# A residual quantizer on one core: the score sums laid out by row group, and the list schedule's numbers that go with it

## The chip, the cores and the metric

The kernel runs on one core of one Trainium2 chip. Time is device time in microseconds (us) of one execution; a kernel's time is the median over its runs. A profiled execution also leaves a trace, in which every instruction of every engine has a start and a duration. The engines are PE (matrix multiply), DVE (vector), ACT (scalar and activations), POOL (used for memsets, small copies and to issue stores) and SP (used to issue loads).

## The reference

The input x has 2 sequences of 16000 rows with 512 bf16 values each. Every row is convolved over time with 3 taps per value and passed through silu. Four quantizer stages follow, each with 8 codes of 512 values: a stage picks the code that is nearest to the residual, adds it to q and takes it from the residual. At the end q is convolved with 3 other taps.

```python
z = silu(sum(xp[:, i:i+T, :] * dw_enc[i] for i in range(3)))
res, q = z, 0
for s in range(4):
    cb = codebooks[s]                                     # 8 x 512
    d2 = sum(res*res)[..., None] - 2 * res @ cb.T + sum(cb*cb)
    sel = cb[d2.argmin(-1)]
    q, res = q + sel, res - sel
y = sum(qp[:, i:i+T, :] * dw_dec[i] for i in range(3))
```

## The kernel before

**Tiles.** A tile is G row groups of 128 partitions, G = 16 for 14 of the 18 tiles and 6 or 8 for the two first and two last. Row p x G + g of the tile is partition p of group g once a row's data lie across the partitions; for the convolution and the residual the 512 values lie on the partitions instead (4 chunks of 128) and the rows along the free dimension (tile ZB).

**Stages of a tile n.** `load` (L456) has SP transpose rows into XT. `front` (L473) multiplies by the taps (L491 on DVE, L490 on ACT), adds (TA, then ZB, both through the helper `tt`, whose instructions all carry L333), and takes exp on ACT (L496) and one plus that on DVE (L498). `front2` (L501) takes the reciprocal on ACT (L508) and multiplies on DVE (ZB<-ZB,EX at L333). `select` (L541) gets from PE, per row, the squared norm and the products with the codes of all stages (L526; read out on DVE at L562 into rr and at L563 into S), and then decides stages 0 to 2 one after another. `resid` (L642) takes the three picked codes off ZB on PE (L661, L662), with the result read out by ACT (L668) or by DVE (L670), then gets the products of the last stage (L688, L689) and decides it (L694 to L699). `windows` (L624) transposes the picks (OHA) on PE (L633) and copies them to OHW (L639). `back` (L704) multiplies OHW by codes that already carry the taps (L721 to L725); ACT reads the result out into YB (L729) and POOL stores it (L752).

**A decision.** For stage s, with shapes of 128 partitions x G row groups x 8 codes:
- PR gets a stage's score without the norm: from S at stage 0 (L573), from RC at stage 1 (L580), from PE's correction in PSUM plus S at stage 2 (L583), and for the last stage as a copy of 8 row groups at a time from PSUM (L689). The arithmetic is f32 in, bf16 out.
- V = PR + the rounded norm (TR at L585, rr3 at L694), bf16 from bf16.
- KEY's upper half-words = V + CCB, the codes' own norms (L588, L696). KEY is f32; its lower half-words hold the code's number, so that no two scores are equal. This instruction writes every second half-word.
- M = the least KEY of each row group (L589, L697), OHA = KEY equal to M (L594, L698).
- For the next stage, PE transposes OHA (L600), ACT or DVE copies that to OT (L604, L605), and PE multiplies it with the codes' products (corr, L610), for RC at L578 or PR at L583; the picked score E (L614, via L333) and its sum RD (L616) update the norm.

PR and V are laid out code by row group: eight runs of GM = 16 values. Instructions that go row group by row group see them through a turned view:

```python
VT, PT = W["V"][:, :, 0:G], W["PR"][:, :, 0:G]                  # [P, C, G], as they lie
V, PR = VT.rearrange("p c g -> p g c"), PT.rearrange("p c g -> p g c")
```

L585 and L694 run in the order in which they lie (the norm then has a step of 1 in the inner loop, over row groups); all others that touch PR or V run through the turned view, with 32 bytes from one code to the next.

**What sets the order.** No engine's order is written out. Each operation is given to `Plan.add` with an engine (or the choice of two), a cost, and a key of stage, tile and place within it. `Plan.order` (L56) is a list scheduler: it keeps a clock for each engine and each PSUM bank and repeatedly takes the operation that could start first by its costs, with ties broken by `rank` (L52), a weighted sum of tile number and place in the stage. WHEN (L213) holds these weights per stage, for first, middle and last tiles (the first 3 and the last 3 are apart). SHARE (L210) shifts the choice between ACT and DVE for the read-out of `resid`, SLACK (L211) for the other operations that either may do (taps, plus 1, OT, OHW). The engines then run their instructions in that order, each waiting for its inputs by semaphores. The scheduler's costs are estimates in the source; the time on the chip doesn't depend on them except through the order.

Of the kernel before, what the change touches and what calls it, by code (L numbers as in the profile page):

```python
# [8 lines left out]
BF16 = mybir.dt.bfloat16  # L9
# [169 lines left out]
def kernel(  # L179
# [8 lines left out]
    nc = tc.nc  # L188
# [18 lines left out]
    PAIR = 1  # L207
    NX, NE, NZ, NOH, NY = 2, 3, 4, 4, 4
    NA = 4
    SHARE = (6.37, 3.09, -1.14)  # L210
    SLACK = (0.29, -1.21, -11.84)  # L211
    QUOTA = {"ACT": 3, "DVE": 4}
    WHEN = {"setup": ((0.48, 0.203), (1.124, 0.191), (0.894, 0.256)), "load": ((-1.978, 0.928), (-1.958, 0.788), (-1.958, 0.928)),  # L213
            "pad": ((-1.401, 0.11), (-1.77, 0.139), (-2.325, 0.134)), "taps": ((-0.057, 0.383), (-0.336, 0.394), (0.031, 0.912)),
            "exp": ((1.263, 0.221), (1.069, 0.366), (0.904, 0.173)), "plus1": ((0.866, 0.996), (0.171, 0.587), (-0.047, 0.932)),
            "recip": ((1.611, 0.712), (1.323, 0), (2.178, 0.449)), "gate": ((0.117, 0.508), (1.051, 0.495), (1.918, 0.485)),
            "score0": ((-0.068, 0.062), (1.311, 0.496), (0.173, 0.112)), "decide": ((1.738, 0.411), (0.985, 0.17), (0.833, 0.78)),
            "win0": ((2.163, 0), (1.992, 0), (2.9, 0.025)), "resid": ((1.585, 0.812), (1.683, 0.698), (1.981, 0.795)),
            "score3": ((2.128, 0.491), (2.581, 0.216), (3.162, 1.381)),
            "decide3": ((0.792, 0.352), (0.868, 0.614), (1.912, 0.464)), "win3": ((2.95, 0.386), (2.949, 1.184), (3.689, 0.225)),  # L220
            "back": ((2.837, 0.461), (3.158, 0.814), (4.316, 0.502))}
    assert B == len(SIZES) and T >= GM * P and GM <= 16

    xf = x.flatten_outer_dims()
# [22 lines left out]
    def sb(shape, dt, name):  # L247
        return const.tile(list(shape), dt, name=name)
# [24 lines left out]
    YB = [sb([P, 4, D], BF16, f"YB{b}") for b in range(NY)]  # L273
    WDBC = YB[3][:, 0:K, :]
    SS = [{"S": sb([P, GM, N3], F32, f"S{b}"), "rr": sb([P, 3, GM, 1], F32, f"rr{b}"), "RD": sb([P, 2, GM, 1], F32, f"RD{b}"),
           "TR": sb([P, 3, GM, 1], BF16, f"TR{b}"), "RC": sb([P, GM, C], F32, f"RC{b}"), "PR": sb([P, C, GM], BF16, f"PR{b}"),
           "V": sb([P, C, GM], BF16, f"V{b}"), "M": sb([P, GM, 1], F32, f"M{b}"), "E2": sb([P, GM, C], F32, f"E2{b}"),
           "OT": [sb([GCM, P], BF16, f"OT{b}_{s}") for s in range(2)],
           "PR3": sb([P, C, GM], BF16, f"PR3{b}"), "rr3": sb([P, GM, 1], BF16, f"rr3{b}"),
           "V3": sb([P, C, GM], BF16, f"V3{b}"), "M3": sb([P, GM, 1], F32, f"M3{b}")} for b in range(2)]  # L280
    PS = [psum.tile([P, 1024], F32, name=f"ps{b}") for b in range(NA)]
    NPART = 3
    BIG = float(2.0 ** 100)
# [257 lines left out]
    def select(st):  # L541
# [1 line left out]
        GC = G * C  # L543
        b = n % 2
        W = SS[b]
        S, M, RC, E2 = W["S"][:, 0:G], W["M"][:, 0:G], W["RC"][:, 0:G], W["E2"][:, 0:G]
        VT, PT = W["V"][:, :, 0:G], W["PR"][:, :, 0:G]
        V, PR = VT.rearrange("p c g -> p g c"), PT.rearrange("p c g -> p g c")
        rr = [W["rr"][:, j, 0:G] for j in range(3)]
        TR = [W["TR"][:, j, 0:G] for j in range(3)]  # L550
        RD = [W["RD"][:, j, 0:G] for j in range(2)]
# [16 lines left out]
        for s in range(3):  # L568
# [6 lines left out]
            else:  # L575
# [6 lines left out]
                else:  # L582
                    add("DVE", small, key(0), lambda pc=pc, cs=cs: nc.vector.tensor_tensor(out=PR, in0=pc(), in1=S[:, :, cs], op=ALU.add),  # L583
                        [("S", b)], [("PR", b)], free=pbox, after=[pj])
            tt(VT, PT, TR[s].rearrange("p g o -> p o g").to_broadcast([P, C, G]), ALU.add, dve(GC, 1.92), key(1), [("PR", b), ("TR", b, s)], [("V", b)])  # L585
            KY = KEY[0]
            k16 = KY.bitcast(BF16).rearrange("p g (c h) -> p g c h", h=2)
            tt(k16[:, 0:G, :, 1], V, CCB[:, :, cs].to_broadcast([P, G, C]), ALU.add, small, key(2), [("V", b), "CCB"], [("KEY", 0)])  # L588
# [35 lines left out]
    def windows(st, s0, s1, key):  # L624
        n, GH = st["n"], st["GH"]
        A, W = OHA[n % NOH], OHW[n % NOH]
        box = {}

        def trans():
            pwb = ps(box).bitcast(BF16)  # L630
            for k in range(GH):
                for s in range(s0, s1):
                    nc.tensor.transpose(pwb[NC * s:NC * (s + 1), k * P:(k + 1) * P],  # L633
                                        A[:, s, 2 * k:2 * k + 4, :].rearrange("p g c -> p (g c)"), IDENT)
        r = slice(NC * s0, NC * s1)
        j = add("PE", 0.5 + GH * 0.0125, key, trans, [("OHA", n % NOH), "I"], [], take=("S", box), mm=GH * (s1 - s0))
        dst = W[r, 0:GH, PADC:PADC + P]
        src = lambda: ps(box).bitcast(BF16)[r, 0:GH * P].rearrange("p (k c) -> p k c", c=P)
        either({"ACT": act_psum(GH * P), "DVE": dve(GH * P, 1.92)}, key, lambda: nc.scalar.copy(dst, src()), lambda: nc.vector.tensor_copy(dst, src()),  # L639
               [], [("OHW", n % NOH, s0 // 3)], free=box, after=[j])  # L640

    def resid(st):  # L642
        n, G, GH = st["n"], st["G"], st["GH"]
        Z, W = ZB[n % NZ], OHW[n % NOH]
        m = 0
        for s in range(3):
            for u in range(2):
                for i in range(KT):
                    box = {}
                    key = ("resid", n, m / 24)  # L650
                    m += 1
                    zg = Z[:, i, u:G:2, :]
                    tok = ("Z", n % NZ, i, u)

                    def mms(s=s, u=u, i=i, zg=zg, box=box):
                        on_act = box["dest"] == "ACT"
                        for k0 in range(0, GH, 4):
                            nk = min(4, GH - k0)
                            o = ps(box)[:, k0 * P:(k0 + nk) * P]
                            if on_act:  # L660
                                nc.tensor.matmul(o, lhsT=IDENT, rhs=zg[:, k0:k0 + nk, :], start=True, stop=False)  # L661
                            nc.tensor.matmul(o, lhsT=CBN[s, u][:, i * P:(i + 1) * P], rhs=W[:, k0:k0 + nk, PADC:PADC + P],  # L662
                                             start=not on_act, stop=True)

                    def evac(zg=zg, box=box):
                        v = ps(box)[:, 0:GH * P].rearrange("p (k c) -> p k c", c=P)
                        if box["dest"] == "ACT":
                            nc.scalar.copy(zg, v)  # L668
                        else:
                            nc.vector.tensor_tensor(out=zg, in0=zg, in1=v, op=ALU.add)  # L670
                    j = add("PE", {"ACT": 2 * mm(GH * P), "DVE": mm(GH * P)}, key, mms, [tok, ("OHW", n % NOH, 0), ("CBN", s, u), "I"], [],
                            take=("A", box), dest="ANY", mm={"ACT": 2 * ((GH + 3) // 4), "DVE": (GH + 3) // 4})
                    add(None, {"ACT": act_psum(GH * P), "DVE": dve(GH * P)}, key, evac, [], [tok], free=box, after=[j])
        b = n % 2
        Q = SS[b]
        rr3, M3 = Q["rr3"][:, 0:G], Q["M3"][:, 0:G]
        PT3, VT3 = Q["PR3"][:, :, 0:G], Q["V3"][:, :, 0:G]
        PR3, V3 = PT3.rearrange("p c g -> p g c"), VT3.rearrange("p c g -> p g c")
        zt = [("Z", n % NZ, i, u) for i in range(KT) for u in range(2)] + [("ZC", n % NZ)]
        nq = len(st["split"])  # L680
        for q, (g0, g1) in enumerate(st["split"]):
            box = {}
            key = ("score3", n, q / nq)
            j = products(st, g0, g1, key, zt + ["MSK", "I"], box)

            def evac(g0=g0, g1=g1, box=box):
                v = view(g0, g1, box)
                nc.vector.tensor_reduce(out=rr3[:, g0:g1, 0], in_=v[:, :, 0:HB], axis=AX.X, op=ALU.max)  # L688
                nc.vector.tensor_copy(PR3[:, g0:g1], v[:, :, HB + N3:])  # L689
            add("DVE", dve((g1 - g0) * (HB + C)) + 0.07, key, evac, [], [("PR3", b), ("rr3", b)], free=box, after=[j])  # L690
        small = dve(G * C)
        key = ("decide3", n, 0)
        cs = slice(N3, NC)
        tt(VT3, PT3, rr3.rearrange("p g o -> p o g").to_broadcast([P, C, G]), ALU.add, dve(G * C, 1.92), key, [("PR3", b), ("rr3", b)], [("V3", b)])  # L694
        k16 = KEY[1].bitcast(BF16).rearrange("p g (c h) -> p g c h", h=2)
        tt(k16[:, 0:G, :, 1], V3, CCB[:, :, cs].to_broadcast([P, G, C]), ALU.add, small, key, [("V3", b), "CCB"], [("KEY", 1)])  # L696
        add("DVE", small, key, lambda: nc.vector.tensor_reduce(out=M3[:, :, 0], in_=KEY[1][:, 0:G], axis=AX.X, op=ALU.min), [("KEY", 1)], [("M3", b)])  # L697
        tt(OHA[n % NOH][:, 3, 1:G + 1, :], KEY[1][:, 0:G], M3.to_broadcast([P, G, C]), ALU.is_equal, small, key, [("M3", b), ("KEY", 1)],  # L698
           [("OHA", n % NOH)])  # L699
        windows(st, 3, 4, ("win3", n, 0))  # L700
# [102 lines left out]
```

## Time and profile before

| | |
|---|---|
| five runs | 741.17, 743.01, 746.38, 746.70, 747.20 us |
| median | 746.38 us |
| profiled execution | 741.17 us |
| its span in the trace | 739.3 us |
| granted PE clock, mean | 0.928 |
| DVE busy in its first 50 us | 41.8 us |
| DVE busy in its last 49.2 us | 32.6 us |

The span runs from the first to the last instruction of the trace; the execution's own time is 1.9 us longer. Busy time is the time in which an engine has at least one instruction under way. In a list of groups a line stands for all instructions with the same line, engine, operation and shapes: their number, busy us in all, mean ns of one, and after the second bar the engine's idle time just before them and what ended it. In a list by time the first column is the start, the second the duration. On DVE the next instruction can start before the one ahead has ended, so that the distance of two starts and the duration are different things.

### The profile page before, as it was taken

How to read it: one execution, taken by the hardware profiler on the slowest of the kernel's cores; microseconds unless marked ns; L12 is line 12 of the kernel's file. 1: busy time of each engine (PE TensorE's matmuls, PEld its weight loads, DVE VectorE, ACT ScalarE, POOL GpSimd, SP SyncE). 2: the span in 40 equal slices, each digit the busy share in tenths (PEclk: the TensorE clock that was granted, in tenths of full speed). 3: DMA queues.
4: the chain of work that ended last, by engine and by line, in shares of the span. 5: the costliest groups of instructions: out<-in, count | busy, mean ns of one | idle time of the engine just before them, and what ended most of it. 6: DMA issues, size and time to landing. Idle time of an engine off the chain costs nothing.

```text
span 739.3 us, 23844 instructions
## 1 busy us (share of the span) xinstructions
PE 539.9 (73%) x10442; PEld 270.7 (37%) x10442; DVE 692.1 (94%) x1250; ACT 667.2 (90%) x591; POOL 129.1 (17%) x199
## 2 busy tenths in 40 slices
PE   1055751787776987797758878877877977998994
PEld 0032330444343444434333434433443433444442
DVE  8979999899999999998999999899999999998892
ACT  7868999899999999898999999799997999998765
POOL 2000023120210313111133001111110031011204
PEclk9997875699999999998989999999997999999998
DMA  5544537425360746639195421918441140212306
GB/s 111 99 93 80 128 61 134 91 34 88 107 123 9 143 81 144 88 64 167 35 159 127 87 58 35 150 49 168 63 75 66 38 123 29 89 57 89 117 9 200
DMA packets 148047, 67.78 MB, mean 92 GB/s; under 512 B 139776, under 2 KB 139808, under 8 KB 147944
## 3 DMA queue, kind: packets, MB, share of 16 engines
q1 hardware_dynamic: 137088, 33.06, 28.3%
q0 software_dynamic: 10640, 32.78, 14.4%
q8 instruction: 81, 1.33, 0.8%
q10 hardware_dynamic: 216, 0.43, 0.2%
q14 instruction: 22, 0.18, 0.1%
HBM read 0.43 MB, written 32.77 MB: 45 GB/s over the span
## 4 chain that ended last, share of the span: by engine, by line
DVE 66%; PE 18%; issue 8%; ACT 4%; SPq 2%; DMA 1%; POOL 0%; DVEq 0%; POOLq 0%; ACTq 0%
DVE ZB L333 13%; DVE ZB L670 12%; DVE TB L491 8%; DVE TA L333 7%; PE ps L526 5%; PE ps L662 4%; PE ps L661 4%; DVE TA L491 4%; DVE EX L498 3%; DVE OHW L639 2%; SPq L462 2%; DVE PR L333 2%; DVE KEY L333 2%; PE ps L721 2%; DVE OHA L333 2%
## 5 line engine op out<-in xcount | busy, mean ns | idle before, releaser
L668 ACT CAST ZB<-ps 128x1024 bf16<-128x1024 f32 (+2 forms) x303 | 259.8, 947 | 39.4 <-PE ps L662 38.0
L662 PE MATMUL ps<-OHW,CBN 128*128 128x512 bf16 (+1 forms) x768 | 267.5, 383 | 19.4 <-DVE ZB L670 8.8
L661 PE MATMUL ps<-ZB,IDENT 128*128 128x512 bf16 (+1 forms) x541 | 209.8, 388 | 27.8 <-DVE ZB L670 19.2
L752 POOL DMA_DIRECT2D out_dram<-YB x130 | 79.1, 613 | 392.8 <-ACT YB L729 374.9
L670 DVE TENSOR_TENSOR ZB<-ZB,ps 128x1024 bf16<-128x1024 bf16 (+2 forms) x129 | 137.0, 1075 | 1.3 <-PE ps L662 0.8
L729 ACT CAST YB<-ps 128x1024 bf16<-128x1024 f32 x126 | 123.1, 1045 | 6.5 <-PE ps L721 5.5
L662 PEld LDWEIGHTS <-CBN 128*128 128x128 bf16 x768 | 75.5, 99 | 141.5 <-issue 72.7
L496 ACT ACTIVATE EX<-ZB 128x4096 bf16<-128x4096 bf16 (+2 forms) x36 | 115.1, 3201 | 4.2 <-DVE ZB L333 4.0
L508 ACT ACTIVATE EX<-EX 128x4096 bf16<-128x4096 bf16 (+2 forms) x36 | 115.3, 3205 | 3.2 <-DVE EX L498 3.0
L526 PE MATMUL ps<-ZB 128*32 128x64 bf16 x8064 | 94.1, 203 | 27.6 <-DVE ZB L333 24.5
L526 PEld LDWEIGHTS <-ZB 128*32 128x32 bf16 x8064 | 81.2, 100 | 84.5 <-issue 62.1
L491 DVE TENSOR_SCALAR TB<-XT,WENC 128x2048 bf16<-128x2048 bf16 (+2 forms) x139 | 95.6, 697 | 0.2
L721 PE MATMUL ps<-WDEC,OHW 128*128 128x512 bf16 x252 | 78.1, 404 | 14.3 <-DVE ZB L670 4.9
L661 PEld LDWEIGHTS <-IDENT 128*128 128x128 bf16 x541 | 53.8, 99 | 64.9 <-issue 12.0
L333 DVE TENSOR_TENSOR ZB<-TA,TB 128x4096 bf16<-128x4096 bf16 (+2 forms) x36 | 74.6, 2072 | 0.7 <-ACT TB L490 0.4
L333 DVE TENSOR_TENSOR ZB<-ZB,EX 128x4096 bf16<-128x4096 bf16 (+2 forms) x36 | 73.4, 2039 | 1.1 <-ACT EX L508 1.1
L333 DVE TENSOR_TENSOR TA<-TA,TB 128x4096 bf16<-128x4096 bf16 (+2 forms) x36 | 73.3, 2037 | 0.3
L468 POOL COPY XT<-XT 128x508 bf16<-128x508 bf16 x18 | 25.2, 1402 | 172.7 <-DMA XT<-in_x_dram 172.7
L491 DVE TENSOR_SCALAR TA<-XT,WENC 128x2048 bf16<-128x2048 bf16 (+2 forms) x70 | 49.6, 721 | 0.3 <-issue 0.2
L633 PE MATMUL ps<-IDENT,OHA 128*32 128x128 bf16 x504 | 25.7, 247 | 24.5 <-DVE PR L689 8.9
L520 PE MATMUL ps<-MSK,IDENT 128*128 128x512 bf16 (+1 forms) x64 | 26.2, 409 | 18.1 <-DVE M L589 3.3
L498 DVE TENSOR_SCALAR EX<-EX 128x4096 bf16<-128x4096 bf16 (+2 forms) x35 | 39.2, 1120 | 0.0
(99 smaller groups left out, 457.2 us busy)
## 6 DMA issues: line engine op xcount, KB each, us to landing
out_dram<-YB POOLq DMA_DIRECT2D x33, 448.0 KB, 3.9
out_dram<-YB POOLq DMA_DIRECT2D x28, 512.0 KB, 4.2
XT<-in_x_dram SPq DMA_TRANSPOSE x252, 3.3
out_dram<-YB POOLq DMA_DIRECT2D x30, 60.0 KB, 4.5
out_dram<-YB POOLq DMA_DIRECT2D x31, 2.0 KB, 3.0
out_dram<-YB POOLq DMA_DIRECT2D x2, 224.0 KB
YB<-in_dw_dec_dram ACTq DMA_DIRECT2D x1, 384.0 KB, 4.0
out_dram<-YB POOLq DMA_DIRECT2D x1, 384.0 KB, 3.7
```

Of the source, the lines that this page charges most:

```text
L333: add("DVE", cost, key, lambda: nc.vector.tensor_tensor(out=out, in0=a, in1=b, op=op), reads, writes, **kw)
L491: lambda dst=dst, src=src, w=w: nc.vector.tensor_scalar(out=dst, in0=src, scalar1=w, scalar2=None, op0=ALU.mult),
L496: add("ACT", act(2 * R), ("exp", n, h), lambda: nc.scalar.activation(v(ex), Z, ACT.Exp, scale=-1.0), zt, [("EX", sl), "ACTTAB"], hold="E")
L508: nc.scalar.add_instruction(mybir.InstActivation(name=nc.get_next_instruction_name(), engine=mybir.EngineType.Activation, func=ACT.Reciprocal,
L526: nc.tensor.matmul(o[HB * q:HB * (q + 1), u * ZW:(u + 1) * ZW].rearrange("p (s c) -> p s c", s=2), lhsT=blk, rhs=both, start=False, stop=( ...
L661: nc.tensor.matmul(o, lhsT=IDENT, rhs=zg[:, k0:k0 + nk, :], start=True, stop=False)
L662: nc.tensor.matmul(o, lhsT=CBN[s, u][:, i * P:(i + 1) * P], rhs=W[:, k0:k0 + nk, PADC:PADC + P], start=not on_act, stop=True)
L668: nc.scalar.copy(zg, v)
L670: nc.vector.tensor_tensor(out=zg, in0=zg, in1=v, op=ALU.add)
L721: nc.tensor.matmul(o, lhsT=W[:, k, PADC:PADC + P], rhs=WDEC[u], start=True, stop=not wrap)
L729: add("ACT", act_psum(1024), key, lambda k=k, box=box, Y=Y, k0=k0: nc.scalar.copy(Y[:, 2 * (k - k0):2 * (k - k0) + 2, :].rearrange("p g d ...
L752: nc.gpsimd.dma_start(out=view[p0:p1, lo:hi, :], in_=Y[p0:p1, lo - g0:hi - g0, :])
```

## The change

PR, V, PR3 and V3 are laid out row group by code in place of code by row group. The turned views go, and the two additions of the norm (L585, L694 before) run row group by row group, with the norm repeated over the 8 codes. The planner is told the cost of such an instruction at the lower rate, two of its other costs are raised, and the numbers SHARE, SLACK and WHEN are new. No operation is added or taken away. In the excerpt, of WHEN only the stages of the decision are shown; the others differ in the same way.

```diff
-    SHARE = (6.37, 3.09, -1.14)
-    SLACK = (0.29, -1.21, -11.84)
+    SHARE = (14.79, 1.9, -1.12)
+    SLACK = (0.29, -1.21, -1.81)
...
-            "score0": ((-0.068, 0.062), (1.311, 0.496), (0.173, 0.112)), "decide": ((1.738, 0.411), (0.985, 0.17), (0.833, 0.78)),
+            "score0": ((-0.15, 0), (1.321, 0.2), (0.126, 0)), "decide": ((1.789, 0.412), (0.54, 0.196), (0.843, 0.939)),
...
-            "decide3": ((0.792, 0.352), (0.868, 0.614), (1.912, 0.464)), "win3": ((2.95, 0.386), (2.949, 1.184), (3.689, 0.225)),
+            "decide3": ((1.618, 0.493), (2.772, 0.723), (3.423, 0.605)), "win3": ((2.988, 0.158), (3.009, 1.183), (3.689, 0.224)),
...
-    "PR": sb([P, C, GM], BF16, f"PR{b}"), "V": sb([P, C, GM], BF16, f"V{b}"),
+    "PR": sb([P, GM, C], BF16, f"PR{b}"), "V": sb([P, GM, C], BF16, f"V{b}"),
...
-    "PR3": sb([P, C, GM], BF16, f"PR3{b}"), "V3": sb([P, C, GM], BF16, f"V3{b}"),
+    "PR3": sb([P, GM, C], BF16, f"PR3{b}"), "V3": sb([P, GM, C], BF16, f"V3{b}"),
...
-            tt(VT, PT, TR[s].rearrange("p g o -> p o g").to_broadcast([P, C, G]), ALU.add, dve(GC, 1.92), key(1), ...)
+            tt(V, PR, TR[s].to_broadcast([P, G, C]), ALU.add, small, key(1), ...)
...
-        j = add("PE", 0.5 + GH * 0.0125, key, trans, ...)
+        j = add("PE", 0.6 + GH * 0.0125, key, trans, ...)
...
-        either({"ACT": act_psum(GH * P), "DVE": dve(GH * P, 1.92)}, key, ...)
+        either({"ACT": act_psum(GH * P), "DVE": dve(GH * P, 1.92) + 0.12 * (s0 == 3)}, key, ...)
...
-        tt(VT3, PT3, rr3.rearrange("p g o -> p o g").to_broadcast([P, C, G]), ALU.add, dve(G * C, 1.92), key, ...)
+        tt(V3, PR3, rr3.to_broadcast([P, G, C]), ALU.add, small, key, ...)
```

More of the change, by code (lines that the diff above doesn't have):

```diff
@@ L209 @@
     NA = 4
-    SHARE = (6.37, 3.09, -1.14)
-    SLACK = (0.29, -1.21, -11.84)
+    SHARE = (14.79, 1.9, -1.12)
+    SLACK = (0.29, -1.21, -1.81)
     QUOTA = {"ACT": 3, "DVE": 4}
[L213 to L216, printed above, removed]
-            "score0": ((-0.068, 0.062), (1.311, 0.496), (0.173, 0.112)), "decide": ((1.738, 0.411), (0.985, 0.17), (0.833, 0.78)),
-            "win0": ((2.163, 0), (1.992, 0), (2.9, 0.025)), "resid": ((1.585, 0.812), (1.683, 0.698), (1.981, 0.795)),
-            "score3": ((2.128, 0.491), (2.581, 0.216), (3.162, 1.381)),
-            "decide3": ((0.792, 0.352), (0.868, 0.614), (1.912, 0.464)), "win3": ((2.95, 0.386), (2.949, 1.184), (3.689, 0.225)),
-            "back": ((2.837, 0.461), (3.158, 0.814), (4.316, 0.502))}
+    WHEN = {"setup": ((0.456, 0.998), (1.178, 0.655), (0.941, 0.735)), "load": ((-1.978, 0.878), (-1.958, 0.738), (-1.958, 0.878)),
+            "pad": ((-1.401, 0.11), (-1.77, 0.139), (-2.325, 0.134)), "taps": ((-0.056, 0.558), (-0.338, 0.569), (0.293, 1.087)),
+            "exp": ((1.265, 0.168), (1.206, 0.297), (1.399, 0.12)), "plus1": ((1.063, 0.361), (0.294, 0.173), (0.161, 0.493)),
+            "recip": ((0.527, 0.735), (0.419, 0.023), (1.274, 0.525)), "gate": ((-0.093, 0.61), (0.842, 0.495), (1.223, 0.636)),
+            "score0": ((-0.15, 0), (1.321, 0.2), (0.126, 0)), "decide": ((1.789, 0.412), (0.54, 0.196), (0.843, 0.939)),
+            "win0": ((2.222, 0), (2.206, 0), (3.035, 0.025)), "resid": ((1.585, 0.81), (1.683, 0.7), (1.984, 0.791)),
+            "score3": ((2.128, 0.749), (2.581, 0.231), (3.178, 1.482)),
+            "decide3": ((1.618, 0.493), (2.772, 0.723), (3.423, 0.605)), "win3": ((2.988, 0.158), (3.009, 1.183), (3.689, 0.224)),
+            "back": ((2.837, 0.37), (3.155, 1.136), (4.316, 0.509))}
     assert B == len(SIZES) and T >= GM * P and GM <= 16
@@ L275 @@
     SS = [{"S": sb([P, GM, N3], F32, f"S{b}"), "rr": sb([P, 3, GM, 1], F32, f"rr{b}"), "RD": sb([P, 2, GM, 1], F32, f"RD{b}"),
-           "TR": sb([P, 3, GM, 1], BF16, f"TR{b}"), "RC": sb([P, GM, C], F32, f"RC{b}"), "PR": sb([P, C, GM], BF16, f"PR{b}"),
-           "V": sb([P, C, GM], BF16, f"V{b}"), "M": sb([P, GM, 1], F32, f"M{b}"), "E2": sb([P, GM, C], F32, f"E2{b}"),
+           "TR": sb([P, 3, GM, 1], BF16, f"TR{b}"), "RC": sb([P, GM, C], F32, f"RC{b}"), "PR": sb([P, GM, C], BF16, f"PR{b}"),
+           "V": sb([P, GM, C], BF16, f"V{b}"), "M": sb([P, GM, 1], F32, f"M{b}"), "E2": sb([P, GM, C], F32, f"E2{b}"),
            "OT": [sb([GCM, P], BF16, f"OT{b}_{s}") for s in range(2)],
-           "PR3": sb([P, C, GM], BF16, f"PR3{b}"), "rr3": sb([P, GM, 1], BF16, f"rr3{b}"),
-           "V3": sb([P, C, GM], BF16, f"V3{b}"), "M3": sb([P, GM, 1], F32, f"M3{b}")} for b in range(2)]
+           "PR3": sb([P, GM, C], BF16, f"PR3{b}"), "rr3": sb([P, GM, 1], BF16, f"rr3{b}"),
+           "V3": sb([P, GM, C], BF16, f"V3{b}"), "M3": sb([P, GM, 1], F32, f"M3{b}")} for b in range(2)]
     PS = [psum.tile([P, 1024], F32, name=f"ps{b}") for b in range(NA)]
@@ L545, in select @@
         W = SS[b]
-        S, M, RC, E2 = W["S"][:, 0:G], W["M"][:, 0:G], W["RC"][:, 0:G], W["E2"][:, 0:G]
-        VT, PT = W["V"][:, :, 0:G], W["PR"][:, :, 0:G]
-        V, PR = VT.rearrange("p c g -> p g c"), PT.rearrange("p c g -> p g c")
+        S, M, V, PR, RC, E2 = W["S"][:, 0:G], W["M"][:, 0:G], W["V"][:, 0:G], W["PR"][:, 0:G], W["RC"][:, 0:G], W["E2"][:, 0:G]
         rr = [W["rr"][:, j, 0:G] for j in range(3)]
@@ L584, in select @@
                         [("S", b)], [("PR", b)], free=pbox, after=[pj])
-            tt(VT, PT, TR[s].rearrange("p g o -> p o g").to_broadcast([P, C, G]), ALU.add, dve(GC, 1.92), key(1), [("PR", b), ("TR", b, s)], [("V", b)])
+            tt(V, PR, TR[s].to_broadcast([P, G, C]), ALU.add, small, key(1), [("PR", b), ("TR", b, s)], [("V", b)])
             KY = KEY[0]
@@ L635, in windows @@
         r = slice(NC * s0, NC * s1)
-        j = add("PE", 0.5 + GH * 0.0125, key, trans, [("OHA", n % NOH), "I"], [], take=("S", box), mm=GH * (s1 - s0))
+        j = add("PE", 0.6 + GH * 0.0125, key, trans, [("OHA", n % NOH), "I"], [], take=("S", box), mm=GH * (s1 - s0))
         dst = W[r, 0:GH, PADC:PADC + P]
         src = lambda: ps(box).bitcast(BF16)[r, 0:GH * P].rearrange("p (k c) -> p k c", c=P)
-        either({"ACT": act_psum(GH * P), "DVE": dve(GH * P, 1.92)}, key, lambda: nc.scalar.copy(dst, src()), lambda: nc.vector.tensor_copy(dst, src()),
+        either({"ACT": act_psum(GH * P), "DVE": dve(GH * P, 1.92) + 0.12 * (s0 == 3)}, key, lambda: nc.scalar.copy(dst, src()), lambda: nc.vector.tensor_copy(dst, src()),
                [], [("OHW", n % NOH, s0 // 3)], free=box, after=[j])
@@ L675, in resid @@
         Q = SS[b]
-        rr3, M3 = Q["rr3"][:, 0:G], Q["M3"][:, 0:G]
-        PT3, VT3 = Q["PR3"][:, :, 0:G], Q["V3"][:, :, 0:G]
-        PR3, V3 = PT3.rearrange("p c g -> p g c"), VT3.rearrange("p c g -> p g c")
+        PR3, rr3, V3, M3 = Q["PR3"][:, 0:G], Q["rr3"][:, 0:G], Q["V3"][:, 0:G], Q["M3"][:, 0:G]
         zt = [("Z", n % NZ, i, u) for i in range(KT) for u in range(2)] + [("ZC", n % NZ)]
@@ L693, in resid @@
         cs = slice(N3, NC)
-        tt(VT3, PT3, rr3.rearrange("p g o -> p o g").to_broadcast([P, C, G]), ALU.add, dve(G * C, 1.92), key, [("PR3", b), ("rr3", b)], [("V3", b)])
+        tt(V3, PR3, rr3.to_broadcast([P, G, C]), ALU.add, small, key, [("PR3", b), ("rr3", b)], [("V3", b)])
         k16 = KEY[1].bitcast(BF16).rearrange("p g (c h) -> p g c h", h=2)
```

## The prediction

> **What bounds the kernel now.** I read the engines' totals first, then the stretch without fill and drain, then the groups that the edit touches, and last the order in time, because a group's mean says how long one instruction lasts and not how long it holds its engine.
>
> The page's head gives the totals of each engine over the profiled execution:
>
> ```profile
> span 739.3 us, 23844 instructions
> PE 539.9 (73%) x10442; PEld 270.7 (37%) x10442; DVE 692.1 (94%) x1250; ACT 667.2 (90%) x591; POOL 129.1 (17%) x199
> ```
>
> The same by engine for 150 to 665 us, where tiles follow each other without a pause (busy us and number of instructions, then clock, DMA share, GB/s):
>
> ```profile
> 150.00:665.00 515.00, 412.14 (x8096) 205.94 (x8094) 500.73 (x846) 486.34 (x386) 85.94 (x115) 0.95 0.44 88
> ```
>
> In the middle DVE is busy 500.7 of 515 us (97.2%) and ACT 486.3 (94.4%). So DVE is the bound, but ACT has only 28.7 us of slack there against DVE's 14.3: time taken from DVE alone soon meets ACT. PE is at 80%.
>
> The groups that the edit touches, and beside them their contiguous likes (busy us, mean ns of one, then idle before):
>
> ```profile
> L333 DVE TENSOR_TENSOR KEY<-V,CCB 128x128 bf16<-128x128 bf16 x56 | 21.7, 388 | 0.0
> L689 DVE CAST PR<-ps 128x64 bf16<-128x64 f32 x30 | 12.6, 419 | 0.0
> L333 DVE TENSOR_TENSOR PR<-S,CCF 128x128 bf16<-128x128 f32 x14 | 10.0, 715 | 0.0
> L333 DVE TENSOR_TENSOR PR<-RC,CCF 128x128 bf16<-128x128 f32 x14 | 9.8, 701 | 0.0
> L333 DVE TENSOR_TENSOR V<-PR,TR 128x128 bf16<-128x128 bf16 x42 | 9.8, 233 | 0.1
> L333 DVE TENSOR_TENSOR E<-S,OHA 128x128 f32<-128x128 f32 x14 | 4.3, 309 | 0.0
> L578 DVE TENSOR_TENSOR RC<-ps,S 128x128 f32<-128x128 f32 x14 | 4.0, 282 | 0.5 <-PE ps L526 0.5
> L343 DVE TENSOR_REDUCE IDH<-IDENT 128x32 f32<-128x128 bf16 x1 | 0.2, 244 | 0.0
> ```
>
> Writing 128 elements to PR takes about 700 ns, while RC, with the same count and even the same input S, takes 282. What differs is the destination: PR is laid out code by row group, and the instruction runs through it row group by row group, so neighbours in its order lie 32 bytes apart. (L583, the third writer of PR, takes 698.)
>
> Then a stretch of DVE's order in time (start, duration; an instruction's end overlaps the next one's start):
>
> ```profile
> 310.62 0.16 DVE L572 CAST TR<-rr 128x16 bf16<-128x16 f32 x1
> 310.70 0.69 DVE L333 TENSOR_TENSOR PR<-S,CCF 128x128 bf16<-128x128 f32 x1
> 311.01 1.43 DVE L670 TENSOR_TENSOR ZB<-ZB,ps 128x1024 bf16<-128x1024 bf16 x1
> 312.36 0.20 DVE L333 TENSOR_TENSOR V<-PR,TR 128x128 bf16<-128x128 bf16 x1
> 312.49 2.27 DVE L333 TENSOR_TENSOR ZB<-ZB,EX 128x4096 bf16<-128x4096 bf16 x1
> 314.69 1.20 DVE L670 TENSOR_TENSOR ZB<-ZB,ps 128x1024 bf16<-128x1024 bf16 x1
> 315.83 0.37 DVE L333 TENSOR_TENSOR KEY<-V,CCB 128x128 bf16<-128x128 bf16 x1
> 316.12 1.20 DVE L670 TENSOR_TENSOR ZB<-ZB,ps 128x1024 bf16<-128x1024 bf16 x1
> ...
> 319.90 0.27 DVE L333 TENSOR_TENSOR E<-S,OHA 128x128 f32<-128x128 f32 x1
> 320.11 0.74 DVE L491 TENSOR_SCALAR TB<-XT,WENC 128x2048 bf16<-128x2048 bf16 x1
> ```
>
> PR lasts 0.69 us but the next one starts 0.31 after it; that next one then lasts 1.43 where its like lasts 1.20. So PR holds DVE for about 0.31 + 0.22 = 0.53 us, not 0.69. E, the contiguous like, holds it for 320.11 - 319.90 = 0.21, V for 0.13, KEY for 0.29. Taking the group means would give a gain nearly twice too large.
>
> [...] IDH reads 128 elements of IDENT 64 bytes apart in 244 ns, no more than GD's contiguous 274 (L403). [...]
>
> **The change part by part**, in time that DVE is held (start to the start of the next; where the next one is slowed, that is added). All are medians of the order in time, 16-group tiles if not said otherwise; there are 14 such tiles and 4 of 6 or 8 groups.
> - PR of the first stage: 0.53 to 0.20, 14 times: -4.6 us. Of the second: 0.50 to 0.20: -4.2. Of the third (L583): 0.43 to 0.20: -3.2. The 12 of small tiles have 48 or 64 elements, so about 0.44 of the mean saving of 0.29: -1.5. Together -13.5. Contiguous f32 to bf16 is not new: OHA<-KEY,M is that, held 0.20.
> - L689, which copies the last stage's 64 elements: 0.13 plus 0.10 on its follower, 0.23 in all, to about 0.13 (OT<-ps copies 128 in 0.14): 32 x 0.10 = -3.2.
> - V: 0.13 to 0.14 before, 0.20 after: 56 x 0.065 = +3.6, and +0.3 for the 16 small ones.
> - KEY reads V, now contiguous. It holds DVE 0.29 where OHA<-KEY,M, as many elements, holds it 0.20. Either the strided read of V costs the 0.09, and then 56 x 0.09 = -5.0; or the write does, which goes to every second half-word and stays. [...] I take the write, so 0: IDH's strided read costs nothing[...]. [...]
> - Sum: -13.5 - 3.2 + 3.9 = -12.8 us of DVE (to -17.8 with KEY). At the lower end, if V costs nothing more, -16.7[...].
> - The decide chain of a tile also gets shorter from start to finish by about 3 x 0.42 - 3 x 0.07 = 1.05 us, but 1 to 4 us between any two of its steps are other DVE work put there by the order (PR at 310.7, V at 312.4, KEY at 315.8), so this is worth something only in the last tile or two: 0 to 1 us.
> - The new list schedule. In the built order ACT gets 301 evictions of ZB for 303 and DVE 131 for 129, ACT four OT copies of full tiles for one; 35 changes between exp and reciprocal in both, so as many table loads; PE one matmul fewer. In DVE time that is 2 x 0.6 + 0.5 - 1.2 - 3 x 0.14, about 0; in ACT time too. The order itself moves many instructions by a few places. No instruction is added, and the queues of SP and POOL keep their items. What it does to waits is open: DVE idled 47 us in all, 8 of it before 50 us and 17 after 690, so some 22 us are in reach of an order. I take 0, and 5 us either way for the range.
>
> **What of it comes off the end.** About 11 of the 14 full tiles lie in the middle, so of 12.8 some 10 us there. DVE then needs 491 us beside ACT's unchanged 486. If DVE stays at 97.2%, the stretch takes 505: -10, and with the rest -12.8. If the two together stay as full as now (987 of 1030), it takes (987 - 10)/987 of 515: -5, and -6.5 in all. With both equally loaded neither covers the other any more, so I go a little below the middle of the two: -9. The profiled execution took 741.2 us, 1.9 more than its span, so 732.2. The runs' median, 746.4, is 0.7% above it (the profiled one was the fastest of five), and 746.4 x 732.2/741.2 = 737.3: forecast 737.
>
> **Rivals.**
> 1. Full value: DVE stays the bound, KEY's excess goes too, and the new order saves a few us: -17.8 - 3 gives 725. For it: 97.2% in the middle. Against: ACT at 94.4%, only 14 us behind. Chance 0.12.
> 2. ACT takes over at once: the DVE time is freed but ACT, whose work is unchanged and which waits 38 us for PE L662, sets the pace, and the gain is 3 us or less: 744. For it: ACT has stretches without a gap (24.62 of 24.68 us from 73.9, 24.63 of 24.66 from 394.2). Against: much of what ACT waits for is PE waiting for DVE (L661 on DVE's ZB, 19.2 us). Chance 0.14.
> 3. The layout isn't what makes PR slow: PR keeps 700 ns, and V adds 3.9: 750. Against: RC and PR share input, count and engine. Chance 0.04.
> 4. Slower through OT on ACT: three more OT copies stand in ACT's order, where one may lie behind a table load (1.28) and an exp or reciprocal (3.63). Corr on PE (L610) waits for it, then RC or PR on DVE, and all DVE work queued behind that. Up to 4.9 each, 14.7 in all, less 9 gained: up to 752. It decides from 3 us lost per copy. Against: the order puts DVE work between OT and RC, 2.6 us of it at the place shown (OT at 320.8, RC at 323.4). Like losses elsewhere in the order count here. Chance 0.10.
>
> **How the numbers follow.** My forecast of -4 to -15 has the remaining 0.60. About 0.5% is what a measurement of this kernel can tell from no change, so faster is below 742.6 and slower above 750.1. Faster: 0.12 + 0.57 + a little of rival 2, 0.71. Slower: half of rivals 3 and 4 and a tail, 0.10. Same: 0.19. The range: below, the full value with KEY and some of the order, 724 (under it 0.07); above, rival 2 and the mild part of rival 4, 747 (over it 0.13).
>
> **What would show it.** PR at about 280 ns and the next start 0.20 after it; the instruction behind PR no longer slowed; V at about 280; KEY at 380 (right) or 280 (the read was it); L689 at about 210. DVE busy near 679 us, ACT near 667, and in the middle both at 95 to 96%. If DVE's busy time falls so and the span doesn't, ACT's or DVE's waits on PE have grown, and the order is to blame. If the span falls by over 18 us, the order gave what I counted at nothing.

## The result, and the profile after

| | before | after |
|---|---|---|
| median | 744.27 us (47 runs) | 741.25 us (26 runs) |
| ratio | | 0.9946, 95% interval 0.993 to 0.9963 |
| profiled execution, its span | 741.17, 739.3 us | 741.57, 739.8 us |
| DVE busy | 692.1 us | 678.6 us |
| ACT busy | 667.2 us | 667.1 us |

The kernel is faster by 0.5%, some 4 us; forecast were 9. A ratio leaves disturbed runs out, so here and below it needn't be the quotient of the two medians. The two profiled executions happen to be equally long (before's is among the shortest of its runs, after's near their median), so the traces tell where time went and not how much was won. They also differ in the clock that PE was granted, a mean of 0.928 in before's and 0.910 in after's, so that a part of a longer wait for PE can be the clock's.

The head of the page of after, and the middle stretch by engine (PE, PE loads, DVE, ACT, POOL, each busy us and instructions; then clock, DMA share, GB/s):

```profile
span 739.8 us, 23855 instructions
PE 543.8 (74%) x10441; PEld 273.0 (37%) x10441; DVE 678.6 (92%) x1249; ACT 667.1 (90%) x592; POOL 129.2 (17%) x199
```

```profile
150.00:665.00 515.00, 415.05 (x8093) 207.59 (x8092) 487.47 (x834) 485.74 (x387) 90.48 (x112) 0.94 0.41 87
```

DVE is 13.5 us less busy, 13.3 of it in the middle, and yet the span is the same: in these two executions the freed time has become idle time. DVE now stands at 94.7% of the middle, where it had 97.2%, and ACT at 94.3%, as before.

The groups of the decision, in after (busy us, mean ns of one, idle before):

```profile
L333 DVE TENSOR_TENSOR KEY<-V,CCB 128x128 bf16<-128x128 bf16 x56 | 17.1, 307 | 0.1
L333 DVE TENSOR_TENSOR V<-PR,TR 128x128 bf16<-128x128 bf16 x42 | 11.8, 280 | 0.0
L685 DVE CAST PR<-ps 128x64 bf16<-128x64 f32 x30 | 6.4, 212 | 0.0
L333 DVE TENSOR_TENSOR PR<-RC,CCF 128x128 bf16<-128x128 f32 x14 | 4.3, 310 | 0.0
L333 DVE TENSOR_TENSOR PR<-S,CCF 128x128 bf16<-128x128 f32 x14 | 3.9, 281 | 0.0
```

and a place in DVE's order (start, duration) like the one shown of before:

```profile
401.12 0.28 DVE L333 TENSOR_TENSOR PR<-S,CCF 128x128 bf16<-128x128 f32 x1
401.33 1.21 DVE L668 TENSOR_TENSOR ZB<-ZB,ps 128x1024 bf16<-128x1024 bf16 x1
402.46 0.28 DVE L333 TENSOR_TENSOR V<-PR,TR 128x128 bf16<-128x128 bf16 x1
402.66 1.21 DVE L668 TENSOR_TENSOR ZB<-ZB,ps 128x1024 bf16<-128x1024 bf16 x1
```

PR lasts 0.28 us and holds DVE for 0.21; the instruction behind it lasts 1.21, its usual time, and not 1.43; V holds DVE 0.20. All as forecast. KEY was to stay at 388 ns and fell to 307 (median 294 over all tiles, where it was 378), and it holds DVE 0.20 where it held 0.29.

What DVE stood idle for shows in its waits, longest in total first (us, times, longest); after, then before:

```profile
DVE ZB L668 <- PE ps L660: 7.3, 8, 1.7
DVE rr L684 <- PE ps L526: 6.1, 6, 1.7
DVE rr L560 <- PE ps L526: 5.5, 6, 2.5
DVE OT L603 <- PE ps L526: 3.5, 4, 1.5
```

```profile
DVE rr L562 <- PE ps L526: 6.6, 5, 2.5
DVE rr L688 <- PE ps L526: 5.5, 6, 1.6
...
DVE ZB L670 <- PE ps L662: 0.8, 3, 0.3
```

Summed over all lines, DVE waits 43.4 us in after against 30.4. Half of the new 13 us is one kind: DVE stands before a read-out of the residual (L668) whose matmul isn't done. Another 4 us are waits for ACT (7.0 against 2.7) and 2 are waits for the products of L526 (21.9 against 19.9). That the order and not the layout is behind them isn't shown by these two pages; the next section takes the two apart.

### The profile page after: what moved, and what is told of

Same layout as the page of the kernel before. It is cut to its first block, busy times and chain, and to the rows that moved or that the text cites. A ratio compares the mean times of both kernels' runs of the same rounds, so it can differ in the third digit from the quotient of the medians.

```text
span 739.8 us, 23855 instructions
## 1 busy us (share of the span) xinstructions
PE 543.8 (74%) x10441; PEld 273.0 (37%) x10441; DVE 678.6 (92%) x1249; ACT 667.1 (90%) x592; POOL 129.2 (17%) x199
## 4 chain that ended last, share of the span: by engine, by line
DVE 49%; PE 28%; issue 8%; ACT 7%; SPq 5%; DMA 1%; POOL 0%; DVEq 0%; POOLq 0%; ACTq 0%
DVE ZB L668 12%; DVE ZB L333 9%; PE ps L660 8%; PE ps L526 7%; PE ps L659 7%; DVE TB L491 6%; SPq L462 5%; DVE TA L333 5%; DVE TA L491 3%; ACT ZB L666 2%; DVE EX L498 2%; PE ps L717 2%; DVE OHW L637 2%; ACT EX L496 2%; PE ps L520 2%
## 5 line engine op out<-in xcount | busy, mean ns | idle before, releaser
L660 PE MATMUL ps<-OHW,CBN 128*128 128x512 bf16 (+1 forms) x768 | 272.5, 391 | 19.2 <-DVE ZB L668 7.8
L659 PE MATMUL ps<-ZB,IDENT 128*128 128x512 bf16 (+1 forms) x540 | 214.4, 397 | 26.8 <-DVE ZB L668 10.4
L668 DVE TENSOR_TENSOR ZB<-ZB,ps 128x1024 bf16<-128x1024 bf16 (+2 forms) x131 | 136.3, 1054 | 8.2 <-PE ps L660 7.3
L748 POOL DMA_DIRECT2D out_dram<-YB x130 | 76.2, 590 | 348.0 <-ACT YB L725 337.4
L526 PE MATMUL ps<-ZB 128*32 128x64 bf16 x8064 | 96.3, 205 | 34.5 <-DVE ZB L333 22.7
L526 PEld LDWEIGHTS <-ZB 128*32 128x32 bf16 x8064 | 82.8, 101 | 89.7 <-issue 67.8
L491 DVE TENSOR_SCALAR TB<-XT,WENC 128x2048 bf16<-128x2048 bf16 (+2 forms) x139 | 92.8, 684 | 0.2
L491 DVE TENSOR_SCALAR TA<-XT,WENC 128x2048 bf16<-128x2048 bf16 (+2 forms) x70 | 47.9, 694 | 0.6 <-DMA XT<-in_x_dram 0.2
L469 POOL COPY XT<-XT 128x508 bf16<-128x508 bf16 x18 | 29.4, 1636 | 78.2 <-DVE TB L491 73.8
L468 POOL COPY XT<-XT 128x508 bf16<-128x508 bf16 x18 | 20.9, 1164 | 123.9 <-DMA XT<-in_x_dram 123.9
L717 PEld LDWEIGHTS <-OHW 128*128 128x128 bf16 x252 | 23.4, 100 | 48.6 <-issue 22.7
```

The lines of the kernel that those rows point to most:

```text
L491: lambda dst=dst, src=src, w=w: nc.vector.tensor_scalar(out=dst, in0=src, scalar1=w, scalar2=None, op0=ALU.mult),
L526: nc.tensor.matmul(o[HB * q:HB * (q + 1), u * ZW:(u + 1) * ZW].rearrange("p (s c) -> p s c", s=2), lhsT=blk, rhs=both, start=False, stop=( ...
L717: nc.tensor.matmul(o, lhsT=W[:, k, PADC:PADC + P], rhs=WDEC[u], start=True, stop=not wrap)
L748: nc.gpsimd.dma_start(out=view[p0:p1, lo:hi, :], in_=Y[p0:p1, lo - g0:hi - g0, :])
```

## The experiments

Two questions were open: what the layout is worth by itself, and what the new order costs or brings. Ratios are to before, run on the same chip at the same time.

### Layout and order apart

The planner's costs are inputs of the order alone, so both halves can be had exactly: the new layout with every engine's order as in before, and the old layout with every engine's order as in after.

```diff
 e1 = before, with
-    "PR": sb([P, C, GM], ...), "V": sb([P, C, GM], ...), "PR3", "V3" likewise
+    "PR": sb([P, GM, C], ...), "V": sb([P, GM, C], ...), "PR3", "V3" likewise
-            tt(VT, PT, TR[s].rearrange("p g o -> p o g").to_broadcast([P, C, G]), ALU.add, dve(GC, 1.92), ...)
+            tt(V, PR, TR[s].to_broadcast([P, G, C]), ALU.add, dve(GC, 1.92), ...)
 e2 = after, with the same lines the other way round and the cost "small" kept
```

> Only the layout is changed; the planner's costs and numbers are those of before, so every engine has the order of before. Theory A (the freed DVE time is worth about 9 us and the new order gave 5 of it back): ratio to before about 0.988, 735 us. Theory B (the freed time is worth only 4 us because ACT, equally loaded, takes over, and the order is neutral): about 0.995, 740 us. Theory C (the order, made for the new layout, is what gains, the layout alone nothing): 1.00, 744 us. DVE busy should be near 678 us in all three, KEY held 0.20 us.

> Only the planner's costs and numbers are those of after; PR and V keep the layout of before, so every engine has the order of after. Theory A: the order costs 5 us on the old layout, 749 us, ratio 1.007. Theory B: 744 us, 1.00. Theory C: the order gains by itself, 740 us or less. DVE busy near 692 us.

Measured: the layout in the old order 0.9781 (0.9751 to 0.9811), 730.4 us; the order on the old layout 1.0093 (1.0064 to 1.0122), 752.5 us. This is theory A, with both sizes larger than it said. On the new layout the new order costs 0.9946/0.9781 = 1.017, 12 us; on the old one 7. The page of the layout in the old order (e1), and its middle stretch:

```profile
span 726.5 us, 23844 instructions
PE 536.1 (74%) x10442; PEld 268.0 (37%) x10442; DVE 675.6 (93%) x1250; ACT 665.4 (92%) x591; POOL 130.7 (18%) x199
```

```profile
150.00:665.00 515.00, 419.03 (x8406) 209.80 (x8405) 494.00 (x869) 494.65 (x394) 91.26 (x120) 0.96 0.44 91
```

DVE's wait for the residual's read-out, in e1 and then in e2, the new order on the old layout:

```profile
DVE ZB L669 <- PE ps L661: 3.6, 7, 1.3
```

```profile
DVE ZB L670 <- PE ps L662: 6.2, 6, 2.1
```

Against 0.8 us before and 7.3 after, most of this wait comes with the order and a smaller part with the layout. A part of the order's price is also work: DVE is busy 678.6 us in after against 675.6 in e1, and 695.4 in e2 against 692.1 before.

In e1 DVE lost 16.5 us of work and the runs 2.2% (1.9 to 2.5, that is 14 to 19 us): most of the freed time, if not all, comes off the end. A rival is the clock that PE was granted. Among the 14 runs of before beside e1, a hundredth less clock goes with 3.3 us more (least squares); e1's median clock was 0.927 and theirs 0.920, so by this estimate the clock makes 2 of the 16 us. The e1 run at 0.920 took 730.9 us. Nor does the clock explain what after loses against e1, since after's median clock, 0.921, is only a little lower.

And ACT, whose work is nearly the same (665.4 us), rose from 94.4% to 96.0% of the middle: its waits fell from 61.6 to 51.3 us in all. This fits ACT waiting for a PE that waits for DVE. The longest wait of ACT and a long one of PE for DVE, before and then in e1:

```profile
ACT ZB L668 <- PE ps L662: 38.0, 51, 3.4
PE ps L661 <- DVE ZB L670: 19.2, 23, 2.0
```

```profile
ACT ZB L667 <- PE ps L661: 30.4, 42, 3.2
PE ps L660 <- DVE ZB L669: 16.4, 20, 1.9
```

### PR alone: which access costs what

```diff
 g1 = before, with only PR and PR3 by row group
-        VT, PT = W["V"][:, :, 0:G], W["PR"][:, :, 0:G]
-        V, PR = VT.rearrange("p c g -> p g c"), PT.rearrange("p c g -> p g c")
+        VT, PR = W["V"][:, :, 0:G], W["PR"][:, 0:G]
+        V, PT = VT.rearrange("p c g -> p g c"), PR.rearrange("p g c -> p c g")
```

> Order of before on every engine. Only PR and PR3 are laid out by row group; V and V3 stay by code, and V is written in the order in which it lies, with PR read 16 bytes apart. If KEY's excess is the strided read of V, KEY stays at 380 ns and DVE is held 0.29 by it; if it was tied to PR's writes it falls to 280. PR falls to 280, L689's copy to 210. V reads with a step[...]; if the strided read costs as KEY's does, 380. DVE saved: 13.5 + 3.2 - 3.9 = 12.8 us, or 7.8 with V at 380; time 732 us (order of before passes the saving on nearly whole) or 737.

Measured 0.9862 (0.983 to 0.9895), 733.5 us. Its groups:

```profile
L333 DVE TENSOR_TENSOR KEY<-V,CCB 128x128 bf16<-128x128 bf16 x56 | 21.8, 392 | 0.0
L333 DVE TENSOR_TENSOR V<-PR,TR 128x128 bf16<-128x128 bf16 x42 | 15.9, 383 | 0.0
L333 DVE TENSOR_TENSOR PR<-S,CCF 128x128 bf16<-128x128 f32 x14 | 4.0, 288 | 0.0
```

and KEY's group in e1, where V is by row group too, with a place in g1's order that shows how long V and KEY hold DVE:

```profile
L333 DVE TENSOR_TENSOR KEY<-V,CCB 128x128 bf16<-128x128 bf16 x56 | 16.7, 300 | 0.0
```

```profile
310.54 0.37 DVE L333 TENSOR_TENSOR V<-PR,TR 128x128 bf16<-128x128 bf16 x1
310.83 2.28 DVE L333 TENSOR_TENSOR ZB<-ZB,EX 128x4096 bf16<-128x4096 bf16 x1
...
314.17 0.38 DVE L333 TENSOR_TENSOR KEY<-V,CCB 128x128 bf16<-128x128 bf16 x1
314.46 1.21 DVE L670 TENSOR_TENSOR ZB<-ZB,ps 128x1024 bf16<-128x1024 bf16 x1
```

With V still by code, KEY keeps its 390 ns, so its excess is the reading of V 32 bytes apart, not its own writes. V itself, which here reads PR 16 bytes apart, takes 383 and holds DVE for 0.29: the strided read makes it as slow as KEY. DVE's busy time, 684.2, is 7.9 us below before's, as the expectation had it for this case (7.8). The time fell further than it had it for this case: 10 us by the ratio (8 to 13), not 7. Here too the clock may have a part: g1's median was 0.930, that of before beside it 0.919, and among those 57 runs a hundredth goes with 2.4 us.

### Which part of the new order

f1, f2 and f3 each take one part of after's planning into e1; every one reshuffles DVE's order, from its 179th (f1), 161st (f2) and 321st instruction (f3) of some 1250 on.

```diff
 f1 = e1, with
+            tt(V, PR, ..., small, key(1), ...)     and V3 likewise
+        j = add("PE", 0.6 + GH * 0.0125, key, trans, ...)
+        either({"ACT": ..., "DVE": dve(GH * P, 1.92) + 0.12 * (s0 == 3)}, key, ...)
 f2 = e1, with WHEN of after
 f3 = e1, with
+    SHARE = (14.79, 1.9, -1.12)
+    SLACK = (0.29, -1.21, -1.81)
```

> New layout; of the planner only the three costs are those of after (V at the lower rate, the picks' transposes on PE 0.1 dearer, the last stage's OHW copy on DVE 0.12 dearer), SHARE, SLACK and WHEN are those of before. Theory P (one set of numbers is bad and the rest harmless): 730 us if the costs are harmless, 740 if they are the bad part. Theory Q (the order of before is a good draw, and any change of the planner's inputs reshuffles it and loses): 735 to 742 here and in the two next runs alike.

> New layout; only WHEN is that of after, costs, SHARE and SLACK are those of before. Theory P: 740 us if WHEN is the bad part, else 730. Theory Q: 735 to 742.

> New layout; only SHARE and SLACK are those of after, costs and WHEN are those of before. Theory P: 740 us if these are the bad part, else 730. Theory Q: 735 to 742.

Measured: 1.0063 (1.0045 to 1.0081), 1.0033 (1.0013 to 1.0053) and 1.0029 (1.0012 to 1.0047); medians 748.8, 747.8, 747.0. No part is harmless, and each alone is worse than all three together (after, 0.9946). That is theory Q, with a larger loss than it said. A part of the loss may be the clock: the medians of the three were 0.909, 0.909 and 0.903 against 0.919 in before's runs beside them, which at 2.4 us per hundredth is 2 to 4 us, where by the ratios they lose 18 to 21 us against e1. Three more runs took steps too small to mean anything, or a single cost:

```diff
 h1 = e1, with
+        j = add("PE", 0.6 + GH * 0.0125, key, trans, ...)
 h2 = e1, with
-    "gate": ((0.117, 0.508), (1.051, 0.495), (1.918, 0.485))
+    "gate": ((0.117, 0.508), (1.06, 0.495), (1.918, 0.485))
 h3 = after, with
-    SHARE = (14.79, 1.9, -1.12)
+    SHARE = (14.79, 1.95, -1.12)
```

> New layout and all of the planner's inputs as before, but for one cost: the picks' transposes on PE are told to take 0.6 in place of 0.5 us. DVE's order is the old one up to its 179th of 1252 instructions and another one from there. Theory Q (the order of before is a good draw, and any other order that the planner makes is a usual one): 743 to 750 us. Theory Q2 (small steps away from the old inputs lose little, and the loss of the three runs before came from many inputs at once): 730 to 736.

> New layout, all of the planner's inputs as before but for WHEN of the gate in the middle tiles, 1.06 for 1.051, a step that means nothing by itself; DVE's order differs from its 225th instruction on. Theory Q: 743 to 750 us. Theory Q2: 730 to 736.

> After, but for SHARE in the middle tiles, 1.95 for 1.9; DVE's order differs from its 334th of 1251 instructions on. Theory Q: the order of after is a better than usual draw too, so 743 to 750 us. Theory Q2: 739 to 743.

Measured: h1 1.0 (0.9977 to 1.0022), h2 1.0013 (0.9998 to 1.0029), h3 0.9936 (0.9913 to 0.996). For the old planner inputs theory Q holds: a step of 0.009 in one weight takes away all that the layout had brought, 2.4% (1.0013/0.9781). For after it doesn't: the one neighbour of its order that was tried is as good as its own. DVE's two longest waits in h2, and the same two in e1:

```profile
DVE rr L686 <- PE ps L526: 14.1, 10, 2.7
DVE ZB L669 <- PE ps L661: 6.6, 11, 1.2
```

```profile
DVE rr L686 <- PE ps L526: 6.5, 5, 3.1
DVE ZB L669 <- PE ps L661: 3.6, 7, 1.3
```

As in f1, the lost time is DVE waiting for PE: 47 us in h2 and 45.5 in f1, against 29.2 in e1, with DVE's work somewhat less (672.7 and 671.9 us against 675.6). For h2 the clock isn't the reason, since its profiled execution had 0.933 and e1's 0.937.

### What holds up after: one engine at a time

```diff
 e3 = after, with
-                            nc.scalar.copy(zg, v)
+                            nc.scalar.copy(zg[:, 0:GH - GH // 8, :], v[:, 0:GH - GH // 8, :])
 e4 = after, with (h = GH - GH // 4)
-                            nc.vector.tensor_tensor(out=zg, in0=zg, in1=v, op=ALU.add)
+                            nc.vector.tensor_tensor(out=zg[:, 0:h, :], in0=zg[:, 0:h, :], in1=v[:, 0:h, :], op=ALU.add)
 h4 = after, with
-            for i in range(KT):
+            for i in range(KT - 1):     in gram, and its stop flag one chunk earlier
```

> After, with ACT's read-out of the residual cut from 8 row-group blocks to 7 (the eighth block's residual is left as it was, so the later picks of those rows differ); same order on all engines. ACT has 239 x 0.107 = 25 us less work. If ACT sets the pace of after: 18 to 25 us less than after, about 718 to 723. If ACT and DVE share the pace: 8 to 12 less, about 731. If the waits on PE set it: 5 or less, 737 or more.

> After, with DVE's read-out of the residual cut from 8 row-group blocks to 6 (two blocks' residual is left as it was, so later picks of those rows differ); same order on all engines. DVE has 97 x 0.267 = 26 us less work. If ACT sets the pace of after: 5 us less or none, 737 or more. If ACT and DVE share the pace: 8 to 12 less, about 731. If DVE is still the bound: 18 to 25 less, about 720.

> After with its order on ACT and DVE, but the products of each row (L526) summed over 3 of the 4 chunks of 128 values, so the scores leave out the last 128 values; PE has 2016 fewer small matmuls, by its busy time of 94 us about 23 us less, all of it ahead of DVE's read-outs that wait on L526 (21.9 us in after). If PE's place in the order is what holds up DVE: 10 to 20 us less than after, 721 to 731. If the waits on PE only hand on what DVE and ACT themselves were late with: 5 less or none, 736 to 741.

e3 and e4 leave out a part of the residual's read-out, h4 a quarter of the products. The busy lines of the three pages, and what came of it:

```profile
PE 534.3 (73%) x10441; PEld 268.5 (37%) x10441; DVE 677.9 (93%) x1249; ACT 646.1 (88%) x592; POOL 144.7 (20%) x199
PE 541.6 (74%) x10441; PEld 271.2 (37%) x10441; DVE 653.9 (89%) x1249; ACT 665.6 (91%) x592; POOL 138.4 (19%) x199
PE 526.8 (72%) x8425; PEld 254.7 (35%) x8425; DVE 675.8 (93%) x1249; ACT 666.2 (91%) x592; POOL 147.0 (20%) x199
```

| | work taken away, by busy time | ratio to before | ratio to after (0.9946) | us off per us of work |
|---|---|---|---|---|
| e3, ACT | 667.1 - 646.1 = 21.0 us | 0.9851 (0.9815 to 0.9887) | 0.990, -7 us | 0.34 |
| e4, DVE | 678.6 - 653.9 = 24.7 us | 0.9824 (0.9792 to 0.9856) | 0.988, -9 us | 0.37 |
| h4, PE | 543.8 - 526.8 = 17.0 us | 0.9857 (0.9816 to 0.9897) | 0.991, -7 us | 0.39 |

The intervals are about 0.35% to each side, some 3 us, so the table can't tell the three apart. In after none of the three engines alone is the bound: whichever is relieved, something comes off the end, but only about a third where the work is ACT's or DVE's. For PE it may be more: h4's runs had a median clock of 0.910 where those of after, e3 and e4 had 0.921 to 0.922, and at the 2.2 us per hundredth that after's own runs show, h4 would gain 9 us, or 0.5 per us of work (an estimate). e4 lies in what was expected if ACT and DVE share the pace, e3 and h4 between two of their expectations. It fits three engines that pass work to each other in a fixed order, each now and then late for another; which waits are passed on wasn't followed one by one.

## Why the prediction was right, and where it was wrong

The time fell within the range and on the forecast side, but about half as far. Three of its terms were wrong, two of them too cautious about the layout and one too kind to the order, and they offset each other: that the time stayed within the range is in part luck.

- **PR, L689, V**: right. PR was to go from 0.43 to 0.53 us held to 0.20, L689 from 0.23 to 0.13, V from 0.13 to 0.20; all three measured so. V's 0.20 was an estimate, from E with as many elements and 0.21 held. That start-to-start time counts and not duration was borne out: added up by the groups' own busy times, the touched instructions lost 27 us from before to e1 (PR 20, L689 6 and KEY 5, while V gained 4), while DVE's busy time fell by 16.5.
- **KEY**: "I take the write, so 0" was wrong. g1 shows that it was the read of V: KEY held DVE 0.29 us there, as in before, and 0.20 in e1; the term measures 56 x 0.09 = -5.0. What I had gone by was a single reduction with one input (IDH, 244 ns with its reads 64 bytes apart, against GD's contiguous 274), and it doesn't carry over to an addition with two; the reason for that stays open. With KEY the sum is -17.8, and e1 measured -16.5. In after DVE's busy time came to the forecast 679 us all the same, because the new order added the 3 us of work that the prediction had put at about 0: that match is luck.
- **"A little below the middle of the two: -9"**, half a DVE bound and half an even share with ACT: wrong in the old order, where most or all came off the end, 16 us. ACT's 94.4% was no second bound: in e1 it reached 96.0% with the same work, which fits that a part of its waits was DVE's lateness passed on by PE. The prediction had this as the argument against rival 2 and then didn't follow it.
- **The order: "I take 0, and 5 us either way"**: the step that failed most. It costs 12 us on the new layout (e1 to after) and 7 on the old. Hence -16 from the layout and +12 from the order gave the -4 measured. The prediction had named the sign of this: DVE's busy time falls, the span doesn't, and waits on PE have grown. But the size was outside its 5 us, and the range held because it reached past the forecast on both sides, not because this was foreseen.
- **Rivals**: the full value (725) was nearly what the layout alone reaches (730). Rival 3 is refuted by PR's 281 ns. Rival 4's own mechanism, DVE held up behind corr by OT copies on ACT, isn't what the waits show: DVE's waits for corr came to 1.4 us in after (L608) and 2.2 before (L610), and the excess lies mostly at the residual's read-out (7.3 us against 0.8). Its wider form, that like losses elsewhere in the order count too, is what happened.

What stays open is why the order of before is so much better than its neighbours. Each part of the changed inputs alone (f1 to f3), one cost alone (h1) and a step that after doesn't have (h2) lose all that the layout had brought, and the share of work between ACT and DVE is the same within 7 us. Whether the old layout too would lose by so small a step wasn't tried; e2 alone says 0.9% for the whole set.

The fastest version that leaves nothing out is e1, the layout of after in the order of before: 0.9781, 730.4 us (five runs). g1, with only PR by row group, beats both kernels as well.

## What to carry to other kernels

Where a planner makes the order, a change of an operation and the new order that comes with it are two changes: hold the order fixed and measure the first alone. Of two steps in the planner's inputs that mean nothing, one moved this kernel by as much as the layout was worth, the other not at all. Count an instruction by how long the next one is held back, its slowing included, not by its duration (PR before: 0.43 to 0.53 us held, 0.70 long). An engine at 94% beside one at 97% isn't necessarily a second bound (ACT went to 96.0% in e1): ask first whether what it waits for is the busier one. Compare the granted clocks before a difference of a few us is put down to the edit (a hundredth went with 2.1 to 3.3 us among the runs of before).

## What was not expected of the hardware

- On DVE the two-input additions that read a bf16 input 16 bytes (V in g1) or 32 bytes apart (KEY before) both held it 0.29 us for 128 elements, against 0.20 where that input was contiguous (V in after, KEY in e1). A one-input reduction that reads 64 bytes apart showed no such cost (IDH before: 244 ns, one instance, against GD's 274 contiguous).
- Writing bf16 32 bytes apart (PR before) cost more than reading so: 0.43 to 0.53 us held where it was 0.20 contiguous (PR in after), and 0.1 to 0.2 of it fell on what came behind (1.43 in place of 1.21 us for a read-out).
